# One strided reduce in place of three maxima, and the floor on 256 values: LSH attention with two gated layers on one Trainium2 core

## The chip, the cores and the metric

The kernel runs on one core of one Trainium2 chip. A core has TensorE (PE; its weight loads are shown apart as PEld), VectorE (DVE), ScalarE (ACT), GpSimd (POOL) and the queue engine SyncE (SP), each with its own list of instructions that it works off in order, waiting on semaphores. The metric is the device time of one execution in microseconds (us).

## The reference

For each of 2 batches and 8 heads there are 768 queries and 768 keys of 64 values. Six signs of a projection give every query and key a bucket; a query attends only to the keys of its own bucket. The result goes through two feed-forward layers.

```python
mask = q_bucket[:, :, :, None] == k_bucket[:, :, None, :]
scores = scale * np.matmul(q, k.transpose(0, 1, 3, 2))
scores = np.where(mask, scores, -1000000000.0)
scores = scores - np.max(scores, axis=-1, keepdims=True)
attn = np.exp(scores)
attn = attn / (np.sum(attn, axis=-1, keepdims=True) + 1e-09)
out = np.matmul(attn, v)                       # (2, 8, 768, 64)
# x: 1536 tokens of 512
g = x @ w_gate; x = (g * sigmoid(g) * (x @ w_val)) @ w_out      # hidden size 1536
h = x @ w_in2; x = (max(h, 0) + alpha * min(h, 0)) @ w_out2     # hidden size 2048
```

## The kernel before

**Work items and units.** An item is a pair of heads and 256 queries; there are 24 (2 batches, 4 pairs, 3 groups of queries). Each item has two units, one for each head: 48 units. Four parts of a unit stand in a fixed order of slots, each part one slot behind the part before it:

- `banks` (`s_bank`, three times): TensorE makes the scores of 768 keys by 256 queries, keys on the partitions, two blocks of 128 keys in each of three PSUM banks. ScalarE copies each bank (L280) into the SBUF tile `se` of 128 partitions by 6 key blocks by 256 queries. Keys of another bucket have a score far below the floor.
- `top` (`s_max`, `s_mt`): VectorE takes the maximum over the 6 key blocks and puts the floor (-1e9, unscaled) under it: L284 (blocks 0 and 1 against 2 and 3, 512 elements in each partition), L285 (blocks 4 and 5 with the floor and with the result, 512 elements) and L287 (the two halves, 256 elements). TensorE transposes the 128 by 256 result (L293), and a reduce of VectorE (L295) takes the maximum over the 128 partitions that are now along the row: 256 maxima, as 128 by 2.
- `back` (`s_mb`, `s_sub`, `s_exp`): TensorE spreads the maxima over the partitions (L300); VectorE puts the floor under the scores and subtracts the maxima in place (L305, 1536 elements); ScalarE takes the exponential (L310).
- `values` (`s_pv`): TensorE multiplies with the values, tile `po` (L317). After the second unit of an item the sums are divided out on VectorE (L333 to L339), and the rows for the first layer are split in two parts (L342 on ScalarE, L346 on POOL).

**The first layer beside it.** After the first 4 items, `stage1` of a group of 256 tokens runs beside the attention of later items: matmuls `gp` and `yp` (L592 to L594), gates on ScalarE and VectorE (L569 to L575), splits on ScalarE (L584) and POOL (L587). Every matmul on a value x is done in three with the high and low part of both operands.

**The weights.** Each of 36 tiles of the first layer (and 32 of the second) is read once as 64-bit floats (`raw`, two buffers) and rounded: ScalarE (L501), VectorE L502 and L504, POOL L506; then ScalarE makes the high part (L530) and VectorE or POOL in turn the low part (L537). For the first group of tokens this lies on the way of `gp`; later groups load the finished tiles (`wb`) from a scratch buffer.

**What sets the order.** The Python code gives an order of recording; a list scheduler then orders each engine's instructions by readiness and by its own costs, and gives out the buffers. So a change of one operation moves others too. `m2` and `m1` have one buffer each, `mq` two, `se` four.

Of the kernel before, what the change touches and what calls it, by code (L numbers as in the profile page):

```python
# [8 lines left out]
F32 = mybir.dt.float32  # L9
# [4 lines left out]
ALU = mybir.AluOpType  # L14
AX = mybir.AxisListType
# [31 lines left out]
def lsh_attention_moe_kernel(  # L47
# [12 lines left out]
    nc = tc.nc  # L60
# [4 lines left out]
    P = 128  # L65
    NC = S // P
    GQ = 256
# [9 lines left out]
    FLOOR = -1.0e9 / SCALE  # L77
# [50 lines left out]
    at = Bag()  # L128
# [151 lines left out]
        nc.scalar.activation(out=u.se[:, 2 * j:2 * j + 2, :], in_=pt, func=AF.Copy)  # L280

    def s_max(u):
        m2 = at.sm.tile([P, 2, GQ], F32, tag="m2", name="m2", bufs=1)
        nc.vector.tensor_tensor(out=m2, in0=u.se[:, 0:2, :], in1=u.se[:, 2:4, :], op=ALU.max)  # L284
        nc.vector.scalar_tensor_tensor(out=m2, in0=u.se[:, 4:6, :], scalar=FLOOR, in1=m2, op0=ALU.max, op1=ALU.max)  # L285
        u.m1 = at.sm.tile([P, GQ], F32, tag="m1", name="m1", bufs=1)
        nc.vector.tensor_tensor(out=u.m1, in0=m2[:, 0, :], in1=m2[:, 1, :], op=ALU.max)  # L287

    def s_mt(u):

        tp = at.ps.tile([P, 2, P], F32, tag=at.tag["m"], name="mt", bufs=at.nb[at.tag["m"]])
        for j in range(2):
            nc.tensor.transpose(tp[:, j, :], u.m1[:, j * P:(j + 1) * P], ident)  # L293
        u.mq = at.sm.tile([P, 2, 1], F32, tag="mq", name="mq", bufs=2)
        nc.vector.tensor_reduce(out=u.mq, in_=tp, axis=AX.X, op=ALU.max)  # L295

    def s_mb(u):
        bc = at.ps.tile([P, 2, P], F32, tag=at.tag["m"], name="mb", bufs=at.nb[at.tag["m"]])
        for j in range(2):
            nc.tensor.transpose(bc[:, j, :], u.mq[:, j, :].to_broadcast([P, P]), ident)  # L300
        u.mx = bc.rearrange("p a b -> p (a b)")
# [58 lines left out]
    def attention():  # L360
# [40 lines left out]
        def top(u):  # L401
            s_max(u)
            s_mt(u)
            step()
            yield
# [331 lines left out]
    k = 0  # L737
# [85 lines left out]
```

## Time and profile before

| | |
|---|---|
| median of 3 runs | 944.47 us (942.78 to 945.28) |
| profiled execution, its own time | 942.76 us |
| its span in the profile | 940.8 us |
| PE, PEld busy | 859.9, 765.6 us |
| DVE, ACT, POOL busy | 593.6, 442.6, 389.3 us |
| mean granted clock of TensorE | 0.967 of 2.4 GHz |

The span is what the profiler saw between the first and the last instruction; 2 us lie around it. Busy time of an engine says how full it was on average over stages that differ, so the rows below are split by stretch: 20 to 60 us (start of the attention), 60 to 240 us (attention beside the first use of the weights), then up to 560 us (attention beside the first layer) and the second layer behind it.

### The profile page before, as it was taken

The numbers are of one execution on the slowest core, as the hardware profiler recorded it, in microseconds if no ns is written. First come the engines' busy times: TensorE is split into PE (matmuls) and PEld (weight loads), VectorE is DVE, ScalarE is ACT, GpSimd is POOL, SyncE is SP. The second block draws the span as 40 slices with busy tenths as digits, with TensorE's granted clock in tenths as the row PEclk, the third lists the DMA queues.
The fourth block names the chain that finished last, engine by engine and source line by source line (L and its number), as shares of the span: only waits on it lengthen the run. The fifth ranks groups of instructions, "written<-read, shape, count | busy, mean of one in ns | idle before, by whom it ended". The sixth has DMA issues, their size and how long they took to land.

```text
span 940.8 us, 14038 instructions
## 1 busy us (share of the span) xinstructions
PE 859.9 (91%) x5248; PEld 765.6 (81%) x5248; DVE 593.6 (63%) x880; ACT 442.6 (47%) x784; POOL 389.3 (41%) x339
## 2 busy tenths in 40 slices
PE   4788787787999999999999997799999999999998
PEld 3577675676898999999999997789887788888886
DVE  4589999998665767677767752131489754335342
ACT  4588565745544554555555441121344433334331
POOL 4224666556433213233223312211478845444442
PEclk8799989989999999999999999899999999999999
DMA  9324767778999767878787867799934010001001
GB/s 236 73 68 134 227 232 218 251 232 268 321 305 298 228 214 242 279 262 280 246 269 235 269 224 290 278 358 362 366 114 155 1 46 1 0 1 45 1 1 45
DMA packets 70403, 180.53 MB, mean 192 GB/s; under 512 B 18880, under 2 KB 25024, under 8 KB 70336
## 3 DMA queue, kind: packets, MB, share of 16 engines
q1 hardware_dynamic: 68176, 174.10, 55.4%
q0 software_dynamic: 2016, 5.51, 2.9%
q8 instruction: 41, 0.67, 0.3%
q14 instruction: 26, 0.21, 0.1%
q10 hardware_dynamic: 144, 0.05, 0.0%
HBM read 152.88 MB, written 26.74 MB: 191 GB/s over the span
## 4 chain that ended last, share of the span: by engine, by line
PE 62%; DVE 16%; DMA 9%; POOL 5%; issue 4%; ACT 4%; SPq 1%; POOLq 0%; DVEq 0%; ACTq 0%
PE po L317 9%; PE gp L592 5%; PE gp L594 5%; PE gp L593 5%; PE hp L594 4%; PE op L599 4%; PE op L597 4%; PE op L598 4%; PE hp L592 4%; PE hp L593 4%; DMA nat<-in_k_dram 3%; DMA raw<-in_wblk_dram 3%; PE yp L594 3%; PE yp L592 2%; PE yp L593 2%
## 5 line engine op out<-in xcount | busy, mean ns | idle before, releaser
L587 POOL TENSOR_TENSOR gl<-ex,gh 128x256 fp32r<-128x256 f32 (+1 forms) x120 | 121.6, 1013 | 265.2 <-ACT gh L584 198.5
L592 PE MATMUL gp<-xh,wb 128*128 128x256 f32 x576 | 177.5, 308 | 18.4 <-ACT wb L530 11.4
L594 PE MATMUL gp<-xh,wb 128*128 128x256 f32 x576 | 168.3, 292 | 6.8 <-POOL wb L537 4.8
L593 PE MATMUL gp<-xl,wb 128*128 128x256 f32 x576 | 166.5, 289 | 1.8 <-POOL xl L346 1.8
L317 PE MATMUL po<-se,vv 128*128 128x256 f32 x576 | 149.8, 396 | 6.5 <-issue 3.5
L592 PEld LDWEIGHTS gp<-xh,wb 128*128 128x128 f32 x576 | 113.1, 196 | 24.7 <-ACT wb L530 14.5
L317 PEld LDWEIGHTS po<-se,vv 128*128 128x128 f32 x576 | 106.6, 199 | 19.8 <-ACT se L310 4.8
L594 PEld LDWEIGHTS gp<-xh,wb 128*128 128x128 f32 x576 | 113.3, 197 | 10.8 <-POOL wb L537 7.0
L593 PEld LDWEIGHTS gp<-xl,wb 128*128 128x128 f32 x576 | 113.5, 197 | 3.0 <-POOL xl L346 2.0
L584 ACT ACTIVATE gh<-ex 128x256 fp32r<-128x256 f32 (+1 forms) x120 | 60.2, 502 | 118.1 <-DVE ex L581 62.5
L310 ACT ACTIVATE se<-se 128x1536 f32<-128x1536 f32 x48 | 71.3, 1484 | 63.5 <-DVE se L305 63.3
L530 ACT ACTIVATE wb<-w 128x512 fp32r<-128x512 f32 x96 | 59.5, 628 | 83.4 <-PE hp L594 55.2
L592 PE MATMUL yp<-gh,wb 128*128 128x256 f32 x288 | 87.3, 305 | 11.6 <-DMA wb<-w 8.1
L537 POOL TENSOR_TENSOR wb<-w,wb 128x512 fp32r<-128x512 f32 x48 | 65.9, 1374 | 74.3 <-ACT wb L530 72.2
L506 POOL TENSOR_TENSOR wt<-wt,wr 128x512 int32<-128x512 int32 x54 | 76.5, 1416 | 48.5 <-DVE wt L504 31.1
L280 ACT ACTIVATE se<-S 128x512 f32<-128x512 f32 x144 | 80.1, 592 | 20.7 <-PE S L279 12.6
L572 DVE SCALAR_TENSOR_TENSOR ex<-ex,gp 128x256 f32<-128x256 f32 x72 | 30.1, 418 | 93.2 <-ACT ex L569 92.7
L537 DVE TENSOR_TENSOR wb<-w,wb 128x512 fp32r<-128x512 f32 x48 | 45.1, 940 | 66.5 <-ACT wb L530 66.5
L305 DVE SCALAR_TENSOR_TENSOR se<-se,mb 128x1536 f32<-128x1536 f32 x48 | 83.8, 1745 | 4.4 <-PE mb L300 4.2
L594 PE MATMUL yp<-gh,wb 128*128 128x256 f32 x288 | 82.2, 291 | 2.7 <-POOL wb L537 1.6
L593 PE MATMUL yp<-gl,wb 128*128 128x256 f32 x288 | 82.0, 286 | 0.5 <-POOL gl L587 0.5
L278 PE MATMUL S<-QA,kt 128*128 128x256 f32 x288 | 78.8, 301 | 1.9 <-ACT se L280 0.9
(92 smaller groups left out, 1943.5 us busy)
## 6 DMA issues: line engine op xcount, KB each, us to landing
wb<-w SPq DMA_DIRECT2D x180, 512.0 KB, 4.9
raw<-in_wblk_dram SPq DMA_DIRECT2D x68, 512.0 KB, 4.4
w<-wb SPq DMA_DIRECT2D x36, 512.0 KB, 5.2
qr<-in_q_dram SPq DMA_DIRECT2D x24, 256.0 KB, 4.4
kt<-in_k_dram POOLq DMA_DIRECT2D x14, 384.0 KB, 8.5
whole<-wt SPq DMA_DIRECT2D x18, 256.0 KB, 2.2
w<-whole SPq DMA_DIRECT2D x18, 256.0 KB, 5.4
nat<-in_k_dram SPq DMA_DIRECT2D x8, 384.0 KB, 7.9
```

The costliest lines, as they stand in the source:

```text
L278: nc.tensor.matmul(pt[:, i, :], lhsT=ka[:, sl], rhs=qa, start=True, stop=False)
L280: nc.scalar.activation(out=u.se[:, 2 * j:2 * j + 2, :], in_=pt, func=AF.Copy)
L305: nc.vector.scalar_tensor_tensor(out=u.se, in0=u.se, scalar=FLOOR, in1=u.mx[:, None, :].to_broadcast([P, NC, GQ]), op0=ALU.max, op1=ALU.su ...
L310: nc.scalar.activation(out=u.se, in_=u.se, func=AF.Exp, scale=SCALE)
L317: nc.tensor.matmul(it.po[:, u.x, :], lhsT=VV[it.b, it.p][:, kb, u.x * D:u.x * D + P], rhs=u.se[:, kb, :], start=kb == 0, stop=kb == NC - 1)
L506: pin(nc.gpsimd.tensor_tensor(out=a, in0=a, in1=r, op=ALU.add))
L537: eng.tensor_tensor(out=ready[i][:, 1, :], in0=wt.pop(i), in1=f32(ready[i])[:, 0, :], op=ALU.subtract)
L584: nc.scalar.activation(out=h, in_=ex, func=AF.Copy)
L587: nc.gpsimd.tensor_tensor(out=l, in0=ex, in1=f32(h), op=ALU.subtract)
L592: nc.tensor.matmul(pt, lhsT=h, rhs=ah, start=first, stop=False)
L593: nc.tensor.matmul(pt, lhsT=h, rhs=al_, start=False, stop=False)
L594: nc.tensor.matmul(pt, lhsT=l, rhs=ah, start=False, stop=last)
```

## The change

The three maxima of a unit (L284, L285, L287) become one reduce on VectorE over a view of `se` with the key blocks innermost: for each of 256 queries it reads 6 values that lie 256 values (1024 bytes) apart, 1536 in all, and writes one. The floor moves behind the transpose and the second maximum: one operation in place on the 256 maxima, 2 in each partition. So the floor goes under the maximum over all 768 keys instead of under a part of it before. The tile `m2` goes, `m1` gets a second buffer. From there on the line numbers are smaller by 2 (by 1 behind the new floor): the new reduce is L285, the floor L294, the subtraction L304.

```diff
     def s_max(u):
-        m2 = at.sm.tile([P, 2, GQ], F32, tag="m2", name="m2", bufs=1)
-        nc.vector.tensor_tensor(out=m2, in0=u.se[:, 0:2, :], in1=u.se[:, 2:4, :], op=ALU.max)
-        nc.vector.scalar_tensor_tensor(out=m2, in0=u.se[:, 4:6, :], scalar=FLOOR, in1=m2, op0=ALU.max, op1=ALU.max)
-        u.m1 = at.sm.tile([P, GQ], F32, tag="m1", name="m1", bufs=1)
-        nc.vector.tensor_tensor(out=u.m1, in0=m2[:, 0, :], in1=m2[:, 1, :], op=ALU.max)
+
+        u.m1 = at.sm.tile([P, GQ], F32, tag="m1", name="m1", bufs=2)
+        nc.vector.tensor_reduce(out=u.m1, in_=u.se.rearrange("p k q -> p q k"), axis=AX.X, op=ALU.max)
...
         nc.vector.tensor_reduce(out=u.mq, in_=tp, axis=AX.X, op=ALU.max)
+        nc.vector.tensor_scalar(out=u.mq, in0=u.mq, scalar1=FLOOR, scalar2=None, op0=ALU.max)
```

VectorE's list at the first unit, which nothing else overlaps (`m_245` is the tile of its maxima, `kt` the keys of the next pair of heads). Before:

```order
L173 TENSOR_TENSOR kt_128<-nat,kt_128 64x768
L284 TENSOR_TENSOR m_245<-se 128x512
L285 SCALAR_TENSOR_TENSOR m_245<-se,m_245 128x512
L287 TENSOR_TENSOR m_248<-m_245 128x256
L295 TENSOR_REDUCE mq<-mt 128x2
L305 SCALAR_TENSOR_TENSOR se<-se,mb 128x1536
```

And with the change:

```order
L173 TENSOR_TENSOR kt_128<-nat,kt_128 64x768
L285 TENSOR_REDUCE m_245<-se 128x256
L293 TENSOR_REDUCE mq<-mt 128x2
L294 TENSOR_SCALAR mq<-mq 128x2
L304 SCALAR_TENSOR_TENSOR se<-se,mb 128x1536
```

The order is the same but for the three that became one (its size is that of its output) and the floor, which stands between the second maximum and the subtraction.

VectorE's list at the ninth unit, where the first weights are rounded (`m_753` before, `m_737` after; L502 and L504 are L501 and L503 after). Before:

```order
L502 TENSOR_SCALAR wt<-raw_556 128x512
L284 TENSOR_TENSOR m_753<-se 128x512
L295 TENSOR_REDUCE mq<-mt 128x2
L504 SCALAR_TENSOR_TENSOR wt<-raw_556,wt 128x512
L305 SCALAR_TENSOR_TENSOR se<-se,mb 128x1536
L285 SCALAR_TENSOR_TENSOR m_753<-se,m_753 128x512
L333 STREAM_TRANSPOSE xf<-den 128x256
L287 TENSOR_TENSOR m_756<-m_753 128x256
```

And with the change:

```order
L501 TENSOR_SCALAR wt<-raw_546 128x512
L304 SCALAR_TENSOR_TENSOR se<-se,mb 128x1536
L503 SCALAR_TENSOR_TENSOR wt<-raw_546,wt 128x512
L285 TENSOR_REDUCE m_737<-se 128x256
L332 STREAM_TRANSPOSE xf<-den 128x256
```

The maximum no longer lies in three pieces between other units' work and the weights' rounding; the reduce stands where the second of the three stood, behind the rounding of the first weight tile.

TensorE's list moves most in items 5 to 10: before the first `po` matmul of item 10 (counted from 0) stand 564 matmuls `gp` and `yp` before and 612 after; at item 11 it is 708 in both. From the `po` of item 11 to the end the two lists are the same but for two rows.

## Rows read from the trace of the kernel before

**Rows 1.** Page: busy tenths in 40 slices of 23.5 us

```profile
PE   4788787787999999999999997799999999999998
...
DVE  4589999998665767677767752131489754335342
```

**Rows 2.** Busy time of each engine by stretch (windows)

```profile
core 0: us, PE busy (x) PEld busy (x) DVE busy (x) ACT busy (x) POOL busy (x), PEclk, DMA share, GB/s
20.00:60.00 40.00, 31.95 (x156) 23.92 (x154) 27.38 (x41) 24.59 (x41) 10.20 (x6) 0.81 0.39 108
60.00:240.00 180.00, 144.31 (x860) 123.91 (x859) 166.28 (x234) 114.05 (x201) 102.37 (x83) 0.92 0.68 215
240.00:300.00 60.00, 56.57 (x398) 52.33 (x399) 36.68 (x60) 28.75 (x54) 20.96 (x22) 0.97 0.99 307
300.00:560.00 260.00, 258.79 (x1909) 248.49 (x1907) 185.97 (x296) 141.84 (x255) 75.04 (x71) 1.00 0.76 254
```

**Rows 3.** The same of instructions on the tiles `m1`, `m2` (windows)

```profile
core 0: us, PE busy (x) PEld busy (x) DVE busy (x), PEclk, DMA share, GB/s
...
60.00:240.00 180.00, 7.04 (x30) 4.14 (x30) 44.02 (x47) 0.92 0.68 215
```

**Rows 4.** VectorE's groups from 60 to 240 us (lines)

```profile
line engine op names shapes xcount | busy us, mean ns | idle before us <-releasers
L504 DVE SCALAR_TENSOR_TENSOR wt<-raw,wt 128x512 int32<-128x512 int32 x35 | 32.7, 934 | 0.1
...
L502 DVE TENSOR_SCALAR wt<-raw 128x512 int32<-128x512 int32 x35 | 24.8, 708 | 0.8 <-DMA raw<-in_wblk_dram 0.7
L285 DVE SCALAR_TENSOR_TENSOR m<-se,m 128x512 f32<-128x512 f32 x16 | 18.2, 1138 | 0.6 <-ACT se L280 0.6
...
L284 DVE TENSOR_TENSOR m<-se 128x512 f32<-128x512 f32 x15 | 15.5, 1033 | 0.4
```

**Rows 5.** Lines by themselves, all calls: duration ns min/median/max, first and last start

```profile
L284 DVE TENSOR_TENSOR m<-se x48: 635/693/1879, 18.8 to 537.2; 128x512 f32<-128x512 f32 x48
...
L285 DVE SCALAR_TENSOR_TENSOR m<-se,m x48: 640/694/2833, 19.6 to 539.0; 128x512 f32<-128x512 f32 x48
...
L305 DVE SCALAR_TENSOR_TENSOR se<-se,mb x48: 1708/1744/1755, 22.8 to 551.4; 128x1536 f32<-128x1536 f32 x48
```

**Rows 6.** Timeline: POOL and VectorE at 113 us

```profile
113.35 1.39 POOL L506 TENSOR_TENSOR wt<-wt,wr 128x512 int32<-128x512 int32 x1 [1.23 <-DVE wt L504]
...
113.71 1.58 DVE L284 TENSOR_TENSOR m<-se 128x512 f32<-128x512 f32 x1
```

**Rows 7.** Chain that ended last, from 60 to 240 us: shares by line

```profile
by line: DVE wt L504 11.8%; issue 10.1%; POOL wt L506 9.7%; DVE se L305 8.1%; DVE wt L502 7.7%; DVE wb L537 6.2%; DVE m L285 6.0%; DVE m L284 4.6%; POOL wb L537 3.8%; ACT wb L530 2.5%; DMA raw<-in_wblk_dram 2.5%; DVE m L287 2.5%; POOL qb L1
```

**Rows 8.** Lines, shapes apart: operations on few elements

```profile
L334 DVE RECIPROCAL r<-xf 128x8 f32<-128x8 f32 x24 | 4.7, 197 | 0.5
...
L108 DVE TENSOR_SCALAR cq<-io 44x1 f32<-44x1 f32 x1 | 0.1, 146 | 0.0
```

**Rows 9.** Lines by themselves: the two that read every second word of `raw`

```profile
L502 DVE TENSOR_SCALAR wt<-raw x54: 384/421/1644, 72.8 to 612.6; 128x512 int32<-128x512 int32 x54
...
L504 DVE SCALAR_TENSOR_TENSOR wt<-raw,wt x54: 644/693/2315, 74.1 to 613.4; 128x512 int32<-128x512 int32 x54
```

**Rows 10.** Timeline: the first unit, from the last copy on

```profile
18.19 1.24 ACT L280 ACTIVATE se<-S 128x512 f32<-128x512 f32 x2 [0.43 <-PE S L279]
18.82 0.69 DVE L284 TENSOR_TENSOR m<-se 128x512 f32<-128x512 f32 x1 [1.68 <-ACT se L280]
19.62 0.69 DVE L285 SCALAR_TENSOR_TENSOR m<-se,m 128x512 f32<-128x512 f32 x1
20.35 0.42 DVE L287 TENSOR_TENSOR m<-m 128x256 f32<-128x256 f32 x1
```

**Rows 11.** Timeline: a unit late in the attention, its last maximum and its transpose

```profile
466.80 0.42 DVE L287 TENSOR_TENSOR m<-m 128x256 f32<-128x256 f32 x1
...
475.36 0.38 PE L293 MATMUL mt<-ident,m 128*128 128x128 f32 x2
```

**Rows 12.** Who waited for whom from 60 to 240 us (us, times, longest)

```profile
ACT wb L530 <- POOL wt L506: 42.0, 27, 3.1
POOL wt L506 <- DVE wt L504: 30.9, 17, 4.0
...
PE gp L592 <- ACT wb L530: 11.4, 10, 2.4
```

**Rows 13.** Timeline: the first values of item 11

```profile
305.25 1.03 PE L317 MATMUL po<-se,vv 128*128 128x256 f32 x4
```

## The prediction, made before the changed kernel ran

> **What bounds the kernel now.** I read the slices of the page first, then the busy time by stretch, then VectorE's groups in the one stretch where VectorE is full, then the chain there. The slices show TensorE near 70 to 80% for the first quarter and near full behind it, with one dip where the attention ends; VectorE is the other way round, full at the start and loose later [rows 1]. In numbers: from 300 to 560 us TensorE works 258.8 of 260 us, so that nothing VectorE saves there can move the end. From 60 to 240 us TensorE works 144.3 of 180 us, VectorE 166.3, POOL 102.4 [rows 2]. In these 180 us the attention and the first rounding of the weights share VectorE. The three maxima of s_max have 44.0 us of them, in 47 instructions, a third of that in units: 15.7 units at 2.81 us each [rows 3]. That is the time which the change touches where it counts.
>
> 2.81 us is more than the work needs. The shortest cases of L284 and L285 take about 0.64 us and their medians 0.69, but the longest 1.88 and 2.83 [rows 5], and in this stretch their means are 1.03 and 1.14 us [rows 4]. The reason stands in the timeline: at 113.35 us POOL starts L506, a sum of two tiles in SBUF, for 1.39 us; L284 starts at 113.71 and takes 1.58 us, and ends 0.55 us behind POOL's [rows 6], nearly the length of its own work. L305, which has three times the elements but reads its second input from PSUM, never takes more than 1.755 us [rows 5]. So an operation of VectorE with two inputs in SBUF waits, in its own time, for a running operation of POOL. The Trainium skill says the same (SBUF — State Buffer, section "Who interferes with whom") and adds that on this chip a reduce never contends with POOL; by that rule the new reduce would show one narrow duration, which no row here can show, since the only reduce before reads PSUM.
>
> **The change part by part.** *Removed:* three instructions a unit. In the stretch 44.0 us; in the late attention more, but hidden.
>
> *Added, the reduce.* 1536 elements from SBUF, one input, 256 values out. Lower bound: L305's 1.744 us for 1536 elements [rows 5]. From L285 (512 elements, 0.694 us) to L305 that is 1.05 us for 1024 elements, 1.025 ns each, with 0.17 us fixed. Upper bound: what a step of 1024 bytes from value to value costs is in no row. The nearest are L502 and L504, which read every second word of `raw`: in their shortest cases they take 0.384 and 0.644 us for 512 elements [rows 9], no longer than L285's on dense data. The farthest is L334, which reads 8 values 128 bytes apart in 0.197 us, 0.051 us above an operation on one value, so at most 7.3 ns for each further one, but that is a reciprocal [rows 8]. I take the first, 1.744 us, because L502 and L504 are the only rows with a step and many elements, and keep twice the price per element (0.17 + 1536 x 2.05 ns = 3.32 us) as the other end.
>
> One rule of the skill speaks against this. The Trainium skill, Vector Engine (DVE) Microarchitecture Reference, section "Measured stream behaviour on trn2", says that a port keeps its rate only on runs of at least two neighbouring words, and gives 1.73 ns per element where one of two sources hops 4 KiB at every element; L502 and L504 have no such runs and yet show no loss. By that figure the reduce would be an estimated 2.83 us, a unit 2.97 us, and the stretch 2.6 us longer. The same section has a case of one source that hops and writes seldom, at the full rate; the reduce is nearer to that one.
>
> *Added, the floor.* 2 elements; the nearest row is L108 at 0.146 us [rows 8]. It stands between the second maximum and the spreading, so it is also 0.15 us in the chain of each unit.
>
> *Sum in the stretch.* A unit goes from 2.81 to 1.744 + 0.146 = 1.89 us, 15.7 units from 44.0 to 29.6 us: 14.4 us less on VectorE. All of it would count if VectorE alone bounded the stretch. The chain that ended last says it does not: L284, L285 and L287 have 4.6 + 6.0 + 2.5 = 13.1% of it, 23.6 of their 44.0 us; POOL's L506 and others stand on it too [rows 7]. By that share 14.4 us become 7.7. I take the middle of 7.7 and 14.4, 11 us.
>
> *POOL and the weights.* The wait goes both ways. L502 and L504 have means of 708 and 934 ns in the stretch [rows 4] against medians of 421 and 693 [rows 9]: 35 x 0.287 + 35 x 0.241 = 18.5 us of waiting that stays. While the reduce runs, POOL can work, so some of this goes as well; if a quarter does, 4.6 us. I put this only into the range, since with VectorE faster the weights' own path (ScalarE waits 42.0 us for POOL's L506, and that 30.9 us for L504) takes more of the time [rows 12].
>
> *Start.* The reduce waits for all three banks. At the first unit L284 begins inside the last copy, at 18.82 us, while this ends at 19.43; L287 ends at 20.77, 1.34 us behind it [rows 10]. The reduce and the floor need 1.89: 0.55 us later. Five units lie before 60 us, where VectorE is two thirds busy and each waits more or less on the last [rows 2]; I put 1 us for them.
>
> *Late attention.* The reduce stands later than L284 did, but behind the last maximum the transpose comes 8 us later [rows 11]; neither the reduce nor a price twice as high gets there. *The order.* Up to item 10 TensorE's list has up to 48 `gp`/`yp` matmuls more in front of the same item, and none from item 11 on: work drawn forward, not added. I cost it at nothing; the cover is VectorE's bound in the stretch, and if the weights are not ready for it, some 10 matmuls' wait, 3 us, come back. *The buffers* of `m1` and the lost `m2` cost nothing: no row names a wait for them.
>
> **Total:** -11 + 1 = -10 us against the profiled execution's 942.8: 932.8. The median of the runs lies 1.7 us above the profiled one, so 934 us is forecast for the median.
>
> **The rivals.** *The stepped read is slow.* Then VectorE, in the stretch where it is full, has more to do and not less. It decides at (2.81 - 0.146 - 0.17) / 1536 = 1.62 ns per element: above that the 44.0 us grow. At twice the dense price a unit is 3.47 us, 15.7 units 54.4 us, 10.4 us more, by the chain's share 5.6, in the middle 8; the five units at the start, each 1.7 us later than their undisturbed 1.81, add about 4: 942.8 + 12 + 1.7 = 956 us. For it: no row shows such a step; against it: rows with a smaller step lose nothing. *The gain is swallowed.* VectorE waits less, but TensorE waits on `wb` of ScalarE and POOL all the same (11.4 us [rows 12]), and 240 to 300 us, with TensorE at 94% and the DMA engines at 0.99 [rows 2], take back what comes earlier: 944 us. Against it: VectorE has 92% of the stretch, and its rounding L504 is first on the chain. *The scheduler's new order* moves the same work about, worth some 3 us either way; it is part of each case's width.
>
> **How the numbers follow.** The full rate with a gain 0.53; the slow read 0.30 (a third of it near the point from which it decides, where the stretch stays as it is and the five first units cost some 0.5 us each, so near 947); swallowed 0.17. 0.3% (2.8 us) is about what a measurement of this kernel can tell from no change. The likeliest case has its own range of 923 to 941: below, 14.4 and 4.6 us in full, less 1 for the start; above, the chain's 7.7 with 3 us lost to the order. The whole range goes up to 955, just short of the doubled price, and leaves out some 0.08 above and 0.06 below. Faster by over 0.3%: 0.53 and a little of the others' width, 0.55. Slower: 0.28. Within: 0.17.
>
> **What would show it.** Right: the reduce at about 1.75 us with hardly any spread, 48 of them; VectorE's time on the maxima in the stretch near 30 us with the floor; the first `po` of item 11, before at 305.3 us [rows 13], some 10 us earlier; from there on the same time to the end. Wrong: a reduce above 2.7 us; or a short reduce and the same start of item 11, with VectorE idle and TensorE waiting for `wb`; or a late transpose that waits for the reduce between 300 and 560 us.

## The result, and the profile after

The changed kernel takes 956.5 us (median of 4 runs, 953.8 to 956.75) against 944.2 us (942.78 to 945.28) for the kernel before: 1.0125 times as long, with a 95% interval of 1.0102 to 1.0148. The forecast was 934 us with 923 to 955 us around it. It is slower, and just outside the range. The profiled execution has a span of 954.9 us, 14.1 more than before.

The page's busy tenths, in 40 slices of 23.9 us [rows 1]:

```profile
PE   4778787777899999999999997889999999999998
...
DVE  5589998989867767877777772221379754335342
```

Busy time by stretch, with the columns of [rows 2]:

```profile
20.00:60.00 40.00, 28.11 (x137) 21.06 (x135) 28.41 (x30) 22.15 (x38) 8.41 (x6) 0.80 0.38 108
60.00:240.00 180.00, 139.60 (x808) 119.92 (x808) 162.65 (x210) 108.60 (x190) 90.65 (x78) 0.91 0.61 202
240.00:300.00 60.00, 55.48 (x408) 51.84 (x407) 43.65 (x59) 31.79 (x60) 25.22 (x26) 1.00 0.98 295
300.00:560.00 260.00, 255.56 (x1875) 242.95 (x1874) 198.87 (x268) 137.99 (x255) 64.32 (x69) 1.00 0.74 251
```

TensorE does less in each of the four, and behind 240 us VectorE does more. The same for the maxima alone [rows 3]:

```profile
60.00:240.00 180.00, 6.12 (x28) 3.44 (x28) 41.46 (x15) 0.91 0.61 202
```

15 reduces in the stretch take nearly what 47 instructions took before; the floor comes on top. The new operations by themselves, in VectorE's groups over the whole run [rows 5, 8]:

```profile
L285 DVE TENSOR_REDUCE m<-se 128x256 f32<-128x1536 f32 x48 | 137.4, 2867 | 21.6 <-ACT se L280 21.5
...
L294 DVE TENSOR_SCALAR mq<-mq 128x2 f32<-128x2 f32 x48 | 17.0, 354 | 0.3
```

And their durations (ns, shortest, median, longest):

```profile
L285 DVE TENSOR_REDUCE m<-se x48: 2751/2870/2956, 16.6 to 553.9; 128x256 f32<-128x1536 f32 x48
```
```profile
L294 DVE TENSOR_SCALAR mq<-mq x48: 132/159/1627, 20.7 to 562.3; 128x2 f32<-128x2 f32 x48
```

The reduce takes 2.87 us and not 1.744. With 0.17 us fixed that is (2.87 - 0.17) / 1536 = 1.76 ns for each element, above the 1.62 at which the first rival decides. It is nearly as steady as was forecast: all 48 cases lie between 2.751 and 2.956 us, and none is long as some of L284 and L285 were. The floor's median of 0.159 us is near the 0.146 that was put down, but its mean is 0.354, because some cases wait: ten of the 48 take more than 0.25 us, and each of these ends some 0.02 to 0.03 us behind the end of an operation of POOL. One of them in the timeline, with the columns of [rows 6]:

```profile
168.09 1.74 POOL L181 TENSOR_TENSOR qb<-qr,QA 64x512 fp32r<-64x512 f32 x1
...
169.05 1.50 DVE L294 TENSOR_SCALAR mq<-mq 128x2 f32<-128x2 f32 x1
...
169.79 0.74 POOL L345 TENSOR_TENSOR xl<-xf,xh 128x256 fp32r<-128x256 f32 x1
```

For 2 elements VectorE stands for 1.5 us while POOL works on tiles in SBUF, through L181 and to the end of L345 behind it (the floor ends at 170.55 us, L345 at 170.53).

Where the 14.1 us lie is seen from the first `po` of two items. In the timelines that of item 4 stands before and after at:

```profile
94.16 1.13 PE L317 MATMUL po<-se,vv 128*128 128x256 f32 x4 [0.32 <-ACT se L310]
```
```profile
100.79 0.92 PE L316 MATMUL po<-se,vv 128*128 128x256 f32 x3 [0.96 <-ACT se L309]
```

That of item 11 stands at 305.25 [rows 13] and at:

```profile
314.65 1.03 PE L316 MATMUL po<-se,vv 128*128 128x256 f32 x4
```

| us | to item 4 | item 4 to 11 | item 11 to the end | span |
|---|---|---|---|---|
| before | 94.2 | 211.1 | 635.5 | 940.8 |
| changed | 100.8 | 213.9 | 640.3 | 954.9 |
| difference | +6.6 | +2.8 | +4.8 | +14.1 |

At the first unit the reduce starts as the last copy ends, at 16.62 us, and takes 2.79 us, where before the maximum was done 1.34 us behind the copy [rows 10]. Who TensorE waited for at its transposes (L291) before 100 us (us, times):

```profile
  DVE m L285: 10.6, 11
  DVE se L304: 6.1, 2
```

These sums count the weight loads' idle time beside the matmuls'. And all that TensorE waited for between 300 and 560 us, where before it was 1.2 us in two waits:

```profile
PE mb L299 <- DVE mq L293: 1.4, 2, 0.7
PE S L278 <- ACT se L280: 0.7, 1, 0.7
PE S L278 <- DVE se L304: 0.6, 1, 0.6
PE hp L189 <- ACT se L280: 0.6, 3, 0.2
PE yp L592 <- POOL gl L586: 0.5, 1, 0.5
```

No transpose waits for a reduce there; it is the spreading behind the second maximum and the floor, and the score matmuls behind late copies and subtractions. These waits are 2.6 us more than before, about half of the 4.8 us that are lost behind item 11.

### The profile page after: what moved, and what is told of

Same layout as the page of the kernel before. It is cut to its first block, busy times and chain, and to the rows that moved or that the text cites. A ratio compares the mean times of both kernels' runs of the same rounds, so it can differ in the third digit from the quotient of the medians.

```text
span 954.9 us, 13949 instructions
## 1 busy us (share of the span) xinstructions
PE 861.6 (90%) x5248; PEld 765.5 (80%) x5248; DVE 622.2 (65%) x832; ACT 439.8 (46%) x784; POOL 373.4 (39%) x339
## 4 chain that ended last, share of the span: by engine, by line
PE 55%; DVE 19%; DMA 9%; ACT 6%; POOL 5%; issue 4%; SPq 1%; POOLq 0%; DVEq 0%; ACTq 0%
PE po L316 6%; DVE m L285 6%; DMA wb<-w 5%; PE gp L593 5%; PE gp L591 5%; PE gp L592 5%; PE hp L593 4%; PE hp L591 4%; PE hp L592 4%; PE op L598 4%; PE op L596 4%; PE op L597 4%; DVE se L304 3%; POOL wt L505 2%; PE yp L593 2%
## 5 line engine op out<-in xcount | busy, mean ns | idle before, releaser
L586 POOL TENSOR_TENSOR gl<-ex,gh 128x256 fp32r<-128x256 f32 (+1 forms) x120 | 117.9, 983 | 274.1 <-ACT gh L583 193.9
L316 PE MATMUL po<-se,vv 128*128 128x256 f32 x576 | 147.8, 393 | 8.5 <-POOL qb L181 4.4
L285 DVE TENSOR_REDUCE m<-se 128x256 f32<-128x1536 f32 x48 | 137.4, 2867 | 21.6 <-ACT se L280 21.5
L505 POOL TENSOR_TENSOR wt<-wt,wr 128x512 int32<-128x512 int32 x54 | 70.9, 1314 | 44.8 <-DVE wt L503 22.1
L304 DVE SCALAR_TENSOR_TENSOR se<-se,mb 128x1536 f32<-128x1536 f32 x48 | 83.7, 1744 | 4.3 <-PE mb L299 4.1
```

What stands on the lines that cost most here:

```text
L285: nc.vector.tensor_reduce(out=u.m1, in_=u.se.rearrange("p k q -> p q k"), axis=AX.X, op=ALU.max)
L304: nc.vector.scalar_tensor_tensor(out=u.se, in0=u.se, scalar=FLOOR, in1=u.mx[:, None, :].to_broadcast([P, NC, GQ]), op0=ALU.max, op1=ALU.su ...
L316: nc.tensor.matmul(it.po[:, u.x, :], lhsT=VV[it.b, it.p][:, kb, u.x * D:u.x * D + P], rhs=u.se[:, kb, :], start=kb == 0, stop=kb == NC - 1)
L505: pin(nc.gpsimd.tensor_tensor(out=a, in0=a, in1=r, op=ALU.add))
L586: nc.gpsimd.tensor_tensor(out=l, in0=ex, in1=f32(h), op=ALU.subtract)
```

## The experiments

Eleven kernels ran, timed (but one) beside the kernel before, whose median was between 942.4 and 943.1 us then, and 944.2 us beside the change itself; so differences between kernels are taken from their ratios to the kernel before, and 0.1% is 0.94 us. "Equal lists" means that every engine has the same operations in the same order in both kernels. Only the changed lines are shown; `...` stands for what is as it was.

**1. The step taken away, everything else as in the change.**

```diff
-        nc.vector.tensor_reduce(out=u.m1, in_=u.se.rearrange("p k q -> p q k"), axis=AX.X, op=ALU.max)
+        nc.vector.tensor_reduce(out=u.m1, in_=u.se.rearrange("p k q -> p (k q)").rearrange("p (a b) -> p a b", b=6), axis=AX.X, op=ALU.max)
```

> The changed kernel with one thing altered: the reduce takes its 1536 values as 256 groups of six neighbours, not as 256 groups of six that lie 1024 bytes apart. So the maxima are over wrongly grouped scores (the shift of the softmax is then another number). Every engine's list is the same, row for row, as in the changed kernel. Theory A (the step between the values costs 0.73 ns for each element): the reduce falls from 2.87 us to about 1.75 us, and the time falls by about 20 us, to 932 to 940 us. Rival B (a reduce in groups of six is slow whatever the step): the reduce stays at 2.87 us and the time at 956 us. Rival C (the scheduler's new order costs the time): the reduce falls to 1.75 us, but the time stays above 950 us.

941.0 us, 0.9973 (0.9957 to 0.9989) of before; the span is 939.5.

```profile
L285 DVE TENSOR_REDUCE m<-se 128x256 f32<-128x1536 f32 x48 | 83.7, 1745 | 28.2 <-ACT se L280 28.1
```

With the lists of all engines alike, the step is worth 1.0125 - 0.9973 = 1.52%, 14.3 us: more than the whole loss, though less than the 20 us that theory A expected, so that the time stays 1 us above its range. Rival B falls, and so does C as the main cause. The new order and the floor, with a reduce as fast as I had put down, are 0.27% (2.5 us) faster than before and not 10 us: something eats most of the gain that was forecast. The stretch of this run, with the columns of [rows 2]:

```profile
60.00:240.00 180.00, 141.71 (x833) 123.24 (x834) 152.50 (x214) 111.95 (x196) 95.54 (x80) 0.91 0.62 208
```

VectorE is down from 166.3 to 152.5 us, and TensorE does no more than before. Its longest waits in the stretch are for weights:

```profile
PE gp L591 <- ACT wb L529: 6.9, 7, 1.7
PE gp L593 <- POOL wb L536: 6.5, 6, 2.0
PE yp L591 <- ACT wb L529: 4.1, 4, 1.7
PE yp L593 <- POOL wb L536: 3.8, 4, 1.2
```

That is 21.3 us, where the same four kinds of wait were 20.0 us before.

**2. No floor.**

```diff
-        nc.vector.tensor_scalar(out=u.mq, in0=u.mq, scalar1=FLOOR, scalar2=None, op0=ALU.max)
```

> The changed kernel without the floor on the 256 maxima; queries without a key in their bucket are left to whatever comes out. Theory A (the step): the floor is 48 small operations whose median is 0.16 us but some wait up to 1.6 us for POOL; without it 1 to 5 us come back, 952 to 956 us. Rival D (the floor, as a wait in VectorE's list and in the chain of each unit, is the loss): back to 942 to 946 us.

948.1 us, 1.0051 (1.0033 to 1.0070) of before. That is 0.74%, 7.0 us less than the change: more came back than theory A gave it, less than D did. The lists are other ones here.

**3. Only the floor moved, the three dense maxima kept.**

```diff
-        nc.vector.scalar_tensor_tensor(out=m2, in0=u.se[:, 4:6, :], scalar=FLOOR, in1=m2, op0=ALU.max, op1=ALU.max)
+        nc.vector.tensor_tensor(out=m2, in0=u.se[:, 4:6, :], in1=m2, op=ALU.max)
...
         nc.vector.tensor_reduce(out=u.mq, in_=tp, axis=AX.X, op=ALU.max)
+        nc.vector.tensor_scalar(out=u.mq, in0=u.mq, scalar1=FLOOR, scalar2=None, op0=ALU.max)
```

> The kernel before with only the second half of the change: three dense maxima as before, the floor not in the second of them but as an operation of its own on the 256 maxima. Theory A: 944 to 949 us, since 48 short operations come on top of an unchanged maximum. Rival D (the floor is the loss): 952 to 957 us. Rival C (any new order costs some 10 us): above 950 us too, but with the floor's own durations short.

941.7 us, 0.9988 (0.9965 to 1.0012): no difference, and below the range of every theory, though the floor is as long as in the change (a mean of 0.42 us, 20.3 us in all). So the floor by itself isn't the loss, and a new order by itself isn't either: D and C fall as sole causes. It does not show that the floor is free: with the floor gone from the second of them, the three maxima took 112.7 us in all and not 126.3, so that VectorE had 13.6 us of the floor's 20.3 back.

**4. What a step costs, on VectorE alone.**

```diff
+        nc.vector.tensor_reduce(out=y[:, :256], in_=step(2), axis=AX.X, op=ALU.max)
...
+        nc.vector.tensor_reduce(out=y[:, :256], in_=cols(6, 256, 256), axis=AX.X, op=ALU.max)
...
```

The two lines are L46, a step of 8 bytes, and L52, a step of 1024.

> Not the program: VectorE alone, four reduces of each kind one behind another over a tile of constants, 1536 elements read in each, and the output is zeros. Groups of six neighbours; two groups of 768 neighbours; six values 8, 16 and 32 bytes apart; six values 1024 and 1040 bytes apart; groups of two 3072 bytes, three 2048 bytes and twelve 512 bytes apart; groups of twelve read as six pairs of neighbours that lie 1024 bytes apart; a two-input maximum with one input stepped by 1024 bytes; and ScalarE's copy of the stepped view beside a dense one. Theory A (a read that hops at every value costs about 1.75 ns for each element and not 1.02): dense groups and pairs 1.75 us, 8 bytes 1.75 us as L502 and L504 let one think, 1024 bytes and the other large steps 2.8 to 2.9 us, with 16 bytes the first that is slow. Rival B (the number of groups costs, not the step): the two groups of 768 are fast, all with 256 groups slow, those with 128 groups between. Rival E (only steps that are a multiple of 1024 bytes collide): 1040 bytes fast.

Groups by line of its one execution, with the columns of [rows 4]:

```profile
L50 DVE TENSOR_REDUCE y<-x 128x256 f32<-128x1536 f32 x4 | 11.6, 2896 | 0.1
L54 DVE TENSOR_REDUCE y<-x 128x256 f32<-128x1536 f32 x4 | 11.5, 2880 | 0.1
L48 DVE TENSOR_REDUCE y<-x 128x256 f32<-128x1536 f32 x4 | 11.4, 2843 | 0.1
L68 ACT ACTIVATE y<-x 128x1536 f32<-128x1536 f32 x4 | 11.2, 2802 | 131.6 <-DVE y L66 131.5
L66 DVE TENSOR_TENSOR y<-x 128x1536 f32<-128x1536 f32 x4 | 11.2, 2799 | 0.1
L52 DVE TENSOR_REDUCE y<-x 128x256 f32<-128x1536 f32 x4 | 11.0, 2739 | 0.1
L60 DVE TENSOR_REDUCE y<-x 128x128 f32<-128x1536 f32 x4 | 10.9, 2724 | 0.1
...
L58 DVE TENSOR_REDUCE y<-x 128x512 f32<-128x1536 f32 x4 | 7.7, 1913 | 0.1
L56 DVE TENSOR_REDUCE y<-x 128x768 f32<-128x1536 f32 x4 | 7.1, 1770 | 0.1
L44 DVE TENSOR_REDUCE y<-x 128x2 f32<-128x1536 f32 x4 | 7.0, 1753 | 0.1
L46 DVE TENSOR_REDUCE y<-x 128x256 f32<-128x1536 f32 x4 | 7.0, 1753 | 0.1
L64 DVE TENSOR_REDUCE y<-x 128x128 f32<-128x1536 f32 x4 | 7.0, 1753 | 0.1
L42 DVE TENSOR_REDUCE y<-x 128x256 f32<-128x1536 f32 x4 | 7.0, 1739 | 0.1
...
L70 ACT ACTIVATE y<-x 128x1536 f32<-128x1536 f32 x4 | 5.9, 1482 | 0.1
```

Always 1536 elements. Six neighbours (L42), two groups of 768 (L44), a step of 8 bytes (L46) and pairs of neighbours 1024 bytes apart (L64) take 1.74 to 1.75 us; steps of 16, 32, 1024 and 1040 bytes (L48, L50, L52, L54) 2.74 to 2.90. Twelve values 512 bytes apart (L60) are slow as well, but two values 3072 bytes apart (L56) cost 1.77 and three at 2048 (L58) 1.91. So neither the number of groups (B) nor a step of just 1024 bytes (E) is it. A step of 8 bytes is free and one of 16 is slow; nothing between was run. From 16 bytes on all are slow but two or three places read in turn. With two it is their number and not the distance: experiment 11 reads two places 1024 bytes apart at the dense price. Three were read at 2048 bytes alone. The slow price holds as well for a maximum with one stepped input (L66) and for ScalarE's copy, 2.80 us against 1.48 (L68, L70).

**5. Neither step nor floor.** The edits of experiments 1 and 2 together.

> The changed kernel with groups of six neighbours (the wrong grouping, as in the first experiment) and without the floor. Its lists are, row for row, those of the run without the floor (948 us). With that run and the two others it makes a square of step and floor. If step and floor add up: 948 less 15 is 933 us. If the floor's waits matter only while VectorE is full: 939 to 942 us, as with the floor. In both, the reduce is 1.75 us.

930.9 us, 0.9882 (0.9842 to 0.9921). Step and floor add up: with the floor the step costs 1.52%, without it 1.0051 - 0.9882 = 1.69% (15.9 us); the floor costs 0.74% beside the stepped reduce and 0.9973 - 0.9882 = 0.91% (8.6 us) beside the dense one. So the floor's price, with the order that comes with it, isn't bound to VectorE being full.

**6. The floor reading PSUM.**

```diff
-        tp = at.ps.tile([P, 2, P], F32, tag=at.tag["m"], name="mt", bufs=at.nb[at.tag["m"]])
+        tq = at.ps.tile([P, 2, GQ], F32, tag=at.tag["m"], name="mt", bufs=at.nb[at.tag["m"]])
+        tp = tq[:, :, :P]
+        raw1 = tq[:, :, P:P + 1]
...
-        nc.vector.tensor_reduce(out=u.mq, in_=tp, axis=AX.X, op=ALU.max)
-        nc.vector.tensor_scalar(out=u.mq, in0=u.mq, scalar1=FLOOR, scalar2=None, op0=ALU.max)
+        nc.vector.tensor_reduce(out=raw1, in_=tp, axis=AX.X, op=ALU.max)
+        nc.vector.tensor_scalar(out=u.mq, in0=raw1, scalar1=FLOOR, scalar2=None, op0=ALU.max)
```

> The changed kernel, its stepped reduce kept, but the 256 maxima go into PSUM and the floor reads them there. If the floor waits for POOL because it reads and writes SBUF, its durations fall from a mean of some 0.45 us and up to 1.6 us to at most 0.25 us, and the time falls part of the way to that without a floor: 948 to 954 us. If something else makes it long, its longest cases stay above 1 us and the time at 955 to 958 us.

952.7 us, 1.0105 (1.0069 to 1.0142). The floor no longer waits:

```profile
L296 DVE TENSOR_SCALAR mq<-mt 128x2 f32<-128x2 f32 x48 | 7.2, 150 | 0.3
```

Its 17.0 us become 7.2, and 0.2% (1.9 us) of time come back, less than the intervals can tell. The lists are other ones again. The next two runs have the lists of this one, but for the floor's own lines, and not those of the change.

**7 and 8. The floor's operation kept, its wait taken away,** with the stepped reduce (first) and with groups of six neighbours (second).

```diff
-        nc.vector.tensor_scalar(out=u.mq, in0=u.mq, scalar1=FLOOR, scalar2=None, op0=ALU.max)
+        nc.vector.tensor_scalar(out=u.mq, in0=tp[:, :, 0:1], scalar1=0.0, scalar2=None, op0=ALU.max)
```

> The changed kernel with its floor operation kept in its place but with its input in PSUM (the first column of the transposed maxima, against zero; so the shift of the softmax is another number, and the floor itself is left out). The lists stay close to those of the changed kernel, closer than in the runs without a floor. If the floor's price is its waiting for POOL: its mean falls from 0.35 us to about 0.16 us, VectorE loses 9 us of busy time over the run, and the time comes to 947 to 951 us. If the price is the place of the operation in VectorE's list and in the chain, or the order that comes with it: 953 to 957 us.

> The kernel of the run above with groups of six neighbours; the lists are the same as there, row for row. With it the step is priced a third time at equal lists: 15 to 17 us less than the run above. If the floor's price is its waiting, 930 to 935 us, as without a floor; if its place or order, 938 to 942 us.

953.4 us, 1.0119 (1.0098 to 1.0141), and 935.5 us, 0.9937 (0.9915 to 0.9958); the second lies between the two ranges that were expected. In both the floor has a mean of 0.149 us. At lists that are the same in the two, the step costs 1.82%, 17.2 us. Against the change and experiment 1, whose lists are other ones, the floor's waits are worth 0.06% beside the stepped reduce, which is nothing that can be told, and 0.36% (3.4 us) beside the dense one; what is left to the runs without a floor, 0.68% and 0.55%, belongs to the operation itself, its place in the chain, or the order that comes with it. Those I could not take apart; experiment 3 does not help, since its maxima became shorter too.

**9. One buffer for `m1`.** In the change `bufs=2` is made 1.

> The changed kernel with one buffer for the 256 by 128 maxima and not two, the part of the change that has no work in it. If the buffers are of no account: 954 to 958 us. If the second buffer hides the wait of a reduce for the transposes of the unit before: above 960 us.

954.6 us, 1.0125 (1.008 to 1.017): the buffers, with the other lists that come with them, are of no account that this interval could tell.

**10. The maxima from PSUM.** A kernel that takes from the prediction that POOL holds up what has two inputs in SBUF: the first two maxima of the kernel before read the banks of scores instead of their copies.

```diff
+            u.pt = []
...
+        u.pt.append(pt)
...
-        nc.vector.tensor_tensor(out=m2, in0=u.se[:, 0:2, :], in1=u.se[:, 2:4, :], op=ALU.max)
-        nc.vector.scalar_tensor_tensor(out=m2, in0=u.se[:, 4:6, :], scalar=FLOOR, in1=m2, op0=ALU.max, op1=ALU.max)
+        nc.vector.tensor_tensor(out=m2, in0=u.se[:, 0:2, :], in1=u.pt[1], op=ALU.max)
+        nc.vector.scalar_tensor_tensor(out=m2, in0=u.pt[2], scalar=FLOOR, in1=m2, op0=ALU.max, op1=ALU.max)
```

> The kernel before with another way out of POOL's way: the first two maxima read banks 1 and 2 of the scores from PSUM and not their copies in SBUF, so that they have one input in SBUF each. If two inputs in SBUF are what waits for POOL, L284 and L285 show at most 0.76 us each and no long cases, and VectorE has some 7 us less from 60 to 240 us; the time is then 936 to 942 us. Against it: the banks come free later, behind VectorE and not behind ScalarE's copy alone, and TensorE may wait for them: 944 to 955 us.

932.2 us, 0.9889 (0.9867 to 0.9910), faster than both kernels and 4 us below the range that was expected, and with the whole of the computation. VectorE's groups over the run:

```profile
L286 DVE TENSOR_TENSOR m<-se,S 128x512 f32<-128x512 f32 x48 | 32.8, 683 | 31.9 <-ACT se L282 31.4
L287 DVE SCALAR_TENSOR_TENSOR m<-S,m 128x512 f32<-128x512 f32 x48 | 32.8, 683 | 7.6 <-ACT se L282 6.9
L289 DVE TENSOR_TENSOR m<-m 128x256 f32<-128x256 f32 x48 | 30.1, 628 | 1.0
```

The two that were 1.03 and 1.14 us in the stretch [rows 4] are at 0.68, and no case of either is above 0.695; only the third, with both inputs in SBUF, still waits. TensorE waits little for a bank that VectorE holds: 1.0 us, once, from 60 to 305 us.

**11. The third maximum as a reduce of two.** As in experiment 10, and:

```diff
-        nc.vector.tensor_tensor(out=u.m1, in0=m2[:, 0, :], in1=m2[:, 1, :], op=ALU.max)
+        nc.vector.tensor_reduce(out=u.m1, in_=m2.rearrange("p k q -> p q k"), axis=AX.X, op=ALU.max)
```

> The kernel with the first two maxima reading PSUM (932 us), and its last maximum, of two halves in SBUF, as a reduce over two values 1024 bytes apart: one input in SBUF, and in VectorE alone two values that far apart cost no more than neighbours. The reduce takes 0.70 us for 512 elements, always, where the maximum of two halves took 0.63 us in the mean with its waits. If POOL's freedom counts: 926 to 931 us. If only VectorE's time counts: 932 to 936 us.

937.6 us, 0.9946 (0.9925 to 0.9967): worse than experiment 10 by 5 us, and above both ranges. The reduce takes 0.692 us, the dense price, as VectorE alone had shown for two places. No gain from leaving POOL free is seen. The 0.064 us more a unit are 3.1 us in all; what the rest of the loss is stays open, since the lists are other ones.

## Why the prediction was wrong, point by point

**The step that failed: the price of the reduce.** "I take the first, 1.744 us, because L502 and L504 are the only rows with a step and many elements." They step by 8 bytes, and 8 bytes is free where the next step that was tried is not: 1.753 us at 8 bytes, 2.843 at 16 (experiment 4). The row was near in kind and on the wrong side of an edge. The reduce takes 2.87 us, and at equal lists that is 14.3 to 17.2 us of time (experiments 1, 5, 7 and 8). On the change's own lists it is 14.3 of the 22 us by which the forecast missed. The rule that was weighed against the trace and put aside had it: the Trainium skill, Vector Engine (DVE) Microarchitecture Reference, section "Measured stream behaviour on trn2", gives 1.73 ns for an element that hops, and the runs show 1.76 in the program and 1.67 alone. The rule as it is worded would have the step of 8 bytes slow too; there it and the measurement differ. The case of the same section that I leaned on, one source read in two places by turns, is right too (1.77 us for two places); six places are not two.

**The sum beside it.** With a reduce at the price that I had put in, the change's own lists take 2.5 us less than before (experiment 1); 10 us less were forecast. Where the floor is at 0.149 us as well, at other lists, it is 0.9937 of before, 5.9 us less (experiment 8), and 11 are got without the floor (experiment 5). So a gain was there, and put 4 to 7 us too high. Inside the sum the parts were off. In the profiled execution of experiment 8 the first `po` of item 4 stands at 99.5 us, 5.3 later than before, where I had put 1; from there to item 11 it takes 201.0 us, 10.1 less than before, where I had 11; from item 11 on 633.0, 2.5 less, where I had nothing. The lower end of the range does not follow from its own terms either: 942.8 - 14.4 - 4.6 + 1 + 1.7 is 926.5 and not 923.

**The floor at 0.146 us.** Its median is right, its mean 0.354 us wrong. L108 ran at the start, alone; the floor meets POOL. I had the mechanism in hand for the other operations and did not look whether it holds for one with a single input. The rows had it: L502, with one input, takes up to 1.644 us at a median of 0.421 [rows 9], and the prediction itself counts that as waiting. It holds for the floor, though the input has 2 elements, and no longer if this lies in PSUM (experiments 6 to 8). The Trainium skill, SBUF — State Buffer, section "Who interferes with whom", counts an operation with one tensor and a number among those that can take the port shared with POOL; the runs agree, with the floor at up to 1.63 us. Some 3.4 us of time at the most hang on the waits; another 5 to 6 us come with the floor as an operation beside a single reduce, or with the other lists, which the sum didn't have and the runs don't explain.

**POOL's hold on two inputs in SBUF,** and that a reduce is free of it, was right: the reduces lie between 2.751 and 2.956 us. Experiment 10 takes the wait from two of the maxima and is faster, at other lists.

**The start.** 1 us was put down and 6.6 came. The five first units each hang on the one before, and TensorE waits at their transposes. The step makes each 1.1 us longer, 5.6 us for five; at equal lists it moves the first `po` of item 4 by 4.2 us (100.8 against 96.6 in experiment 1) and by 7.3 (106.8 against 99.5 in experiments 7 and 8). So these units should have been counted about in full. With the dense price 2.4 and 5.3 us are left, where five units at the 0.08 us of the sum would be 0.4. That rest stays open: these are single executions, and their granted clock up to 100 us lay between 0.85 and 0.93.

**The late attention.** "Neither the reduce nor a price twice as high gets there" was right of the transpose and wrong as a conclusion: 4.8 us are lost behind item 11, where TensorE waits at the spreading and the scores. With the dense reduce, at equal lists, this part is 633.2 us (experiment 1), and the loss is gone. With only the floor's waits taken away it is 636.2 (experiment 7); so the floor seems to have a share too, but there the lists are other ones.

**The rivals.** The first came true in its mechanism: its place, its price above 1.62 ns. Its 956 us is the measured number, but by compensation: it was worked out at 3.32 us a reduce. At the measured 2.87 the same sum gives a unit of 3.02 us, 3.3 us more in the stretch, 2.5 of them counted, 3 at the start, and 950 us; it has no term for the floor's waits and the late attention, and 3 us too little for the start. The second rival, the swallowed gain, looks like experiment 1: VectorE 13.8 us less busy in the stretch, 2.5 us of time saved, and TensorE waiting for `wb` as long as before. Its mechanism is not shown, though: experiment 8 has as much of these waits (24.8 us in all, from ScalarE and POOL, against 21.3) and gets its gain. What eats the rest in experiment 1, beside the floor's waits, stays open.

## What to carry to other kernels

Before a chain of dense operations is folded into one with a strided view, price the stride in the smallest kernel that has it: six values in turn, 1536 in all, cost 1.75 us with neighbours or a step of 8 bytes and 2.7 to 2.9 us at the steps from 16 bytes on, and that is more than the three maxima take undisturbed (1.81 us). Not only an operation with two inputs in SBUF can wait for POOL in its own time: the floor, one input and two elements, did so too, while the reduces did not. With the input, or one of two, in PSUM the wait was gone, and used on the maxima themselves this came with 1.1% less time. A row of the trace bounds a price only if it lies on the same side of the edge as the new operation.

## What the runs showed of the hardware that was not expected

- A stepped read of a few places in turn is cheap: two places 3072 bytes apart 1.77 us, three at 2048 bytes 1.91, but six at 1024 bytes 2.74 and twelve at 512 bytes 2.72, each for 1536 elements (experiment 4). In pairs of neighbours the hop is free (1.753 us).
- ScalarE pays it too: a copy of 1536 elements is 1.48 us dense and 2.80 us stepped by 1024 bytes.
- An operation on 2 elements stood up to 1.63 us in VectorE behind POOL, and with its input in PSUM between 0.119 and 0.161 us (experiments 6 to 8).
- TensorE's mean granted clock was between 0.964 and 0.985 in the profiled executions of the whole program, and the two fastest kernels have the highest (0.985, experiments 5 and 10); from 60 to 240 us it was 0.92 before and 0.96 to 0.97 in these two. It is not what makes experiment 10 faster: its four executions have 0.971 to 0.985 and take 930.7 to 934.0 us, and those of the kernel before with as high a clock take 938.4 to 946.1. Why the clock is higher there the runs do not tell.
